# Decode attention with a parallel ReLU FFN: V on a second DMA queue, and weights instead of activations held stationary in the output products

## The chip, the cores and the metric

The kernel runs on one core of one Trainium2 chip. The metric is the device time of one execution in microseconds; the time before is the median of 3 runs. Lower is better.

## The reference

```python
x  = A_x                                   # (2, 1, 512) bf16
xn = layernorm(x)
q  = (xn @ wq).reshape(2, 1, 32, 128).transpose(0, 2, 1, 3)
s  = einsum("bhqd,bhkd->bhqk", q, k_cache) * 128 ** -0.5     # k_cache (2, 32, 8192, 128)
p  = softmax(s, axis=-1)
o  = einsum("bhqk,bhkd->bhqd", p, v_cache)
attn = o.transpose(0, 2, 1, 3).reshape(2, 1, 4096) @ wo      # wo (4096, 512)
ffn  = maximum(xn @ w1, 0) @ w2                              # w1 (512, 1792), w2 (1792, 512)
return x + attn + ffn                                        # (2, 1, 512) bf16
```

One token for each of 2 batch rows attends over 8192 cached keys in 32 heads. K and V are 128 MiB each, the weights 4 + 4 + 3.5 MiB. Everything is bf16.

## The kernel before, in words

The 64 (batch, head) combinations are taken in 32 pairs. One pair's K is one transfer of 4 MiB: 128 partitions, 64 for each head of the pair, each partition with 128 consecutive keys (32 KiB). V is laid out the same way. There are two buffers for K (`ks`) and two for V (`vs`); pair t uses buffer t % 2.

A step of PE (`step`, lines 337 to 361) does, for pair t: wait for K(t) (`dK`); 16 groups of 8 transposes of K tiles into PSUM (`tp`, L301); each group is copied to SBUF (`kT`, L416) by ACT (groups in `ON_ACT`) or DVE, and two groups later PE multiplies it with the pair's q (scores, L308, 64 moving columns). Then PE does the weighted sum with V of the pair before (`weighted`, L321), while DVE and ACT form the maximum and the exponentials of pair t. The first such sum, in pair 0, runs over a zero `prm`. ACT's part of a step (`pair`, lines 527 to 546) is: the kT copies, the maximum to SBUF (L533), two Exp activations with sums (L537), and, when PE has finished the weighted sum (`sW`), the copy of the result to `OTf` (L525). ACT runs its 32 pairs as a rolled loop of 16 rounds with two pairs each.

All large transfers are issued from SP's queue (lines 181 to 203), in this order: wq (L177, into `vs[1]`), w1, w2, K0, K1, V0; then, for t = 0 to 29: wait until PE has done the transposes of pair t, issue K(t+2); wait until PE has done the weighted sum of step t (`sW`), issue V(t+1). At last V31 in two halves (L196), wo in five pieces of 14, 7, 6, 3 and 2 blocks (L201, into the space of w1 and w2), and the store of the result (L166).

The prologue computes the layernorm, q (L247), FFN1 (L260, w1 stationary) and FFN2 (L278): there the ReLU result `hT` is stationary, 32 columns wide with the two batch rows 16 columns apart and zeros between, and w2 moves; the four 128-wide blocks of the output go to four column groups of the PE array, PSUM partitions 0, 32, 64, 96. Four more matmuls (L286) add x through `onex`, and the sum is kept in `ys` (128x128).

The tail, after step 31: row sums of the exponentials through `onesh` (L376), the weighted sum of V31 half by half (L321), division (L497, L501), transposes (L386), a selection product that puts o into the order of wo's rows (L391) and the copy to `OX` (L508), then wo (L405) in the same form as FFN2: `OX` stationary, 32 columns wide, wo moving, four column groups. DVE adds `ys` (L512), and SP stores 8 rows that lie 16 partitions apart.

Of the kernel before, what the change touches and what calls it, by code (L numbers as in the profile page):

```python
# [7 lines left out]
ALU = mybir.AluOpType  # L8
# [3 lines left out]
R = 2  # L12
# [7 lines left out]
def kernel(  # L20
# [13 lines left out]
    P = 128  # L34
    HP = P // 2
    bf16 = mybir.dt.bfloat16
    f32 = mybir.dt.float32

    Bsz, Sq, D = A_x.shape
# [3 lines left out]
    KT = D // P  # L43
# [3 lines left out]
    NP = N // 2  # L47
    WJ = H * Dh // P
# [8 lines left out]
    FJ = FT  # L57
    inv_sqrt = float(Dh) ** -0.5
    eps = 1e-5

    CT = P // KT
    CB = CT // Bsz
    assert KT * Bsz * CB == P
    ctx.enter_context(tc.tile_critical(no_gpsimd_drain=True))

    def sb(shape, dt, name):
        return ctx.enter_context(nc.sbuf_tensor(name, shape, dt))
# [14 lines left out]
    wo_sb = w_sb[:, 0:WJ * D].rearrange("p (j n) -> p j n", j=WJ)  # L82
    kT = [sb([P, EG, P], bf16, f"kT{i}") for i in range(4)]
    identb = sb([P, P], bf16, "identb")
    sel = sb([H, DQ, P], bf16, "sel")
    onesh = sb([P, 2, P], f32, "onesh")
    onesb = sb([1, P], bf16, "onesb")
# [19 lines left out]
    RD = sb([P, N], f32, "RD")  # L107
    OTn = sb([P, Bsz, H], bf16, "OTn")
    Ob = sb([H, Bsz, Dh], bf16, "Ob")
    OX = sb([P, WJ, CT], bf16, "OX")  # L110
    hT = sb([P, FJ, CT], bf16, "hT")
    ys = sb([P, P], f32, "ys")
    osb = sb([P, P], bf16, "osb")
    onex = sb([Bsz, CT], bf16, "onex")

    tp = [ps([P, EG, P], bf16, f"tp{i}") for i in range(4)]
    Sc = [ps([P, 512], f32, f"Sc{i}") for i in range(2)]
# [37 lines left out]
        "p (kt b) -> p kt b", b=Bsz  # L155
    )
    hp = ot[1][:, 0:FJ * Bsz].rearrange("p (j b) -> p j b", b=Bsz)
    y = Sc[1][:, 0:P]
    fin = ot[0][:, 0:P]

    def cols(ap, c):
        return ap[c * CT:(c + 1) * CT, :]


    def store(eng):
        eng.dma_start(  # L166
            out.rearrange("b s (c p) -> c (b s) p", p=P),
            osb[0:P - CB + 1:CB, :],
        ).then_inc(dO, 16)

    def load_k(t):
        nc.sync.dma_start(ks[t % R][:], K_all[t * P:(t + 1) * P, :]).then_inc(dK[t % R], 16)
# [1 line left out]
    def load_v(t):  # L174
        nc.sync.dma_start(vs[t % R][:], V_all[t * P:(t + 1) * P, :]).then_inc(dV[t % R], 16)
# [5 lines left out]
    @(lambda f: f(nc.sync))  # L181
    def _(sp):
        sp.dma_start(w1_sb, B_w1.rearrange("(p kt) f -> p kt f", kt=KT)).then_inc(dW1, 16)  # L183
        sp.dma_start(w2_sb, B_w2.rearrange("(p j) n -> p j n", j=FJ)).then_inc(dW2, 16)  # L184
        load_k(0)
        load_k(1)
        load_v(0)
        for t in range(NP - 2):
            sp.wait_ge(pT[NG - 1], t + 1)
            load_k(t + R)  # L190
            sp.wait_ge(sW, t + 1)
            load_v(t + 1)
        sp.wait_ge(sW, NP - 1)
        for i in range(2):
            sl = slice(i * SLOT // 2, (i + 1) * SLOT // 2)
            sp.dma_start(  # L196
                vs[(NP - 1) % R][:, sl], V_all[(NP - 1) * P:NP * P, sl]
            ).then_inc(dH[i], 16)
        for c in range(NC):
            sl = slice(cuts[c], cuts[c + 1])  # L200
            sp.dma_start(wo_sb[:, sl, :], wo_v[:, sl, :]).then_inc(dW[c], 16)  # L201
        sp.wait_ge(sE, 1)
        store(sp)


    @(lambda f: f(nc.gpsimd))
    def _(g):
        g.memset(identb[:], 0.0).then_inc(sG, 1)
        g.memset(sel[:], 0.0).then_inc(sG, 1)
        g.memset(onesh[:], 0.0).then_inc(sG, 1)  # L210
        g.wait_ge(sG, 1)
        g.affine_select(
            out=identb[:], in_=identb[:], compare_op=ALU.not_equal, fill=1.0,
            base=0, pattern=[[-1, P]], channel_multiplier=1,
        ).then_inc(sI, 1)
        g.wait_ge(sG, 2)
        g.affine_select(
            out=sel[:], in_=sel[:], compare_op=ALU.not_equal, fill=1.0,
            base=0, pattern=[[-1, DQ], [1, P]], channel_multiplier=-DQ,
        ).then_inc(sI, 1)  # L220
        g.wait_ge(sI, 2)
        g.memset(prm[0][:], 0.0).then_inc(sG, 1)
        g.wait_ge(sG, 4)
        for u in range(2):
            g.memset(onesh[u * HP:(u + 1) * HP, u, :], 1.0).then_inc(sI, 1)
            g.wait_ge(sI, 3 + u)
        g.memset(OX[:], 0.0).then_inc(sI, 1)
        g.wait_ge(sV, 100)
        for t in range(NP):
            if t >= R:  # L230
                g.wait_ge(sS, t - R + 1)
            g.tensor_copy(q2[t % R][:], qb[:, 2 * t:2 * t + 2]).then_inc(sQ1, 1)  # L232
        g.wait_ge(dO, 16).then_inc(sG, 1)
# [3 lines left out]
    def _(pe):  # L237
# [36 lines left out]
        pe.wait_ge(sF, 2)  # L274
        pe.wait_ge(dW2, 16)
        for j in range(FJ):
            for c in range(KT):
                pe.matmul(  # L278
                    cols(y, c),
                    lhsT=hT[:, j, :],  # L280
                    rhs=w2_sb[:, j, c * P:(c + 1) * P],
                    start=(j == 0),
                    stop=False,
                )
        for c in range(KT):
            i = pe.matmul(  # L286
                cols(y, c),
                lhsT=onex[:],
                rhs=xsb[:, c * P:(c + 1) * P],
                start=False,  # L290
                stop=True,
            )
        i.then_inc(sF, 1)

# [80 lines left out]
        for u in range(2):  # L375
            t = pe.matmul(dbp[:, :, u], lhsT=onesh[:, u, :], rhs=RS[:], start=True, stop=True)  # L376
        t.then_inc(sH, 1)
        for i in range(2):
            pe.wait_ge(dH[i], 16)
            for e in range(i * NG // 2, (i + 1) * NG // 2):  # L380
                weighted(1, e)
# [19 lines left out]
        for c in range(NC):  # L401
            pe.wait_ge(dW[c], 16)
            for j in range(cuts[c], cuts[c + 1]):
                for k in range(KT):
                    t = pe.matmul(  # L405
                        cols(fin, k),
                        lhsT=OX[:, j, :],
                        rhs=wo_sb[:, j, k * P:(k + 1) * P],
                        start=(j == 0),
                        stop=(j == WJ - 1),  # L410
                    )
        t.then_inc(sH, 1)

    def kcopy(eng, e):
        fn = eng.copy if e in ON_ACT else eng.tensor_copy
# [4 lines left out]
    def _(v):  # L420
        v.memset(eps_t[:], eps).then_inc(sV, 1)
        v.memset(onesb[:], 1.0)
        v.memset(xz[:], 0.0).then_inc(sZ, 1)
        v.memset(onex[:], 0.0)
        v.memset(hT[:], 0.0).then_inc(sZ, 1)
        v.memset(prm[R - 1][:], 0.0).then_inc(sP, 1)
        v.wait_ge(dX, 16)
        v.bn_stats(out=stats[:], in_=xsb[:]).then_inc(sV, 1)
# [12 lines left out]
            op1=ALU.mult,  # L441
        ).then_inc(sV, 1)
        v.wait_ge(sQ, 1)
        v.wait_ge(sI, 1)
        v.wait_ge(sZ, 1)
        v.tensor_copy(xz[:, :, Z:Z + Bsz], tpx).then_inc(sV, 1)
        v.wait_ge(sQ, 2)
# [1 line left out]
        v.tensor_scalar(  # L449
            out=qs[:], in0=qp, scalar1=inv_sqrt, scalar2=None, op0=ALU.mult  # L450
        ).then_inc(sV, 1)
        v.wait_ge(sZ, 2)
        v.tensor_copy(onex[:, 0:CT:CB], identb[0:Bsz, 0:Bsz])
        v.wait_ge(sF, 1)
        v.tensor_scalar(
            out=hT[:, :, 0:CT:CB], in0=hp, scalar1=0.0, scalar2=None, op0=ALU.max,
        ).then_inc(sF, 1)
        v.wait_ge(sQ, 3)

# [2 lines left out]
            tpq.rearrange("p l (g b) -> p l g b", b=Bsz),  # L462
        ).then_inc(sV, 93)
        v.wait_ge(sF, 3)
        v.tensor_copy(ys[:], y).then_inc(sF, 1)

        def pair(i, n):
            for e in range(NG):
# [18 lines left out]
        with v.Fori(0, NP // R):  # L487
# [16 lines left out]
        v.wait_ge(sH, 2)  # L504
        v.tensor_copy(Ob[:], tp[0][0:H, 0:Bsz, :]).then_inc(sV, 1)
        v.wait_ge(sH, 3)
        v.wait_ge(sI, 5)
        v.tensor_copy(  # L508
            OX[:, :, 0:CT:CB], Sc[1][:, 0:Bsz * WJ].rearrange("p (b j) -> p j b", b=Bsz)
        ).then_inc(sV, 1)  # L510
        v.wait_ge(sH, 4)
        v.tensor_tensor(out=osb[:], in0=fin, in1=ys[:], op=ALU.add).then_inc(sE, 1)  # L512


    @(lambda f: f(nc.scalar))
    def _(a):
        a.wait_ge(sV, 3)
        a.activation(
            out=rstd[:], in_=mv[:, 1:2], func=ACTF.Sqrt, bias=eps_t[:Bsz], scale=1.0
        ).then_inc(sA, 1)  # L520


        def out_copy(r, n, c):
            a.wait_ge(sW, n)
            a.copy(OTf[:, bass.ds(c, 2)], ot[r][:, 0:2]).then_inc(sO, 1)  # L525

        def pair(i, n, t):
            for e in range(NG):
                if e in ON_ACT:
                    a.wait_ge(pT[e], n)  # L530
                    kcopy(a, e)
            a.wait_ge(sB, n)
            a.copy(nm[i][:], bc_of(i)).then_inc(sN, 1)  # L533
            a.wait_ge(sN, n)
            for u in range(2):
                half = slice(u * HP, (u + 1) * HP)
                x = a.activation(  # L537
                    out=prm[i][half, :, u],
                    in_=S_of(i)[half, :, u],
                    func=ACTF.Exp,  # L540
                    bias=nm[i][half, u:u + 1],
                    scale=1.0,
                    accum_out=RS[half, bass.ds(t, 1)],
                )
            x.then_inc(sP, 1)
            out_copy(1 - i, n, t * 2)

        a.copy(nm[0][:, 0:1], eps_t[:]).then_inc(sO, 1)
        reg = nc.alloc_register(mybir.EngineType.Activation, "pairno_a")
        a.reg_mov(reg, 0)  # L550
        with a.Fori(0, NP // R) as tr:
            for r in range(R):
                a.reg_add(reg, reg, 1)
                pair(r, reg, tr * R + r)
# [1 line left out]
_INS = ['A_x', 'A_k_cache', 'A_v_cache', 'A_wq', 'A_wo', 'B_x', 'B_w1', 'B_w2']  # L556
_OUTS = [((2, 1, 512), 'bfloat16')]
# [25 lines left out]
```

## Time and profile before

| what | us |
|---|---|
| median of 3 runs (662.2 to 662.62) | 662.31 |
| the profiled execution's own time | 662.31 |
| its span in the profile | 660.24 |
| PE busy in the span | 557.1 |
| PE weight loads busy | 535.8 |
| DVE busy | 254.1 |
| ACT busy | 255.8 |
| mean granted TensorE clock | 0.935 |

An engine's busy time is the sum of its instructions' times in the span; PE and its weight loads overlap. The page cuts the span into 40 slices of 16.5 us and gives for each the busy share of the engines, of the 16 DMA engines, and the bytes moved. The timeline gives rows of "start us, duration us, engine, line, operation, out<-in, count", and in brackets how long the engine had been idle and what ended that. "SPq" and "ACTq" are DMA issues from the queue of that engine.

### The profile page before, as it was taken

Reading aid. Unit: us, or ns where it says so; the run is one execution under the profiler, and the core shown is the slowest. Engines: PE = TensorE matmul, PEld = TensorE weight load, DVE = VectorE, ACT = ScalarE, POOL = GpSimd, SP = SyncE. Lnnn points to the kernel's source line nnn. Section 1 sums busy time; section 2 is a strip of 40 time slices with the busy share of each in tenths; the row PEclk is TensorE's granted clock in tenths of the full one; section 3 lists DMA queues with packets and bytes.
Section 4 is the critical chain, followed back from the end, with each engine's and each line's share of the span. In section 5 each row is a group of like instructions: output and inputs, shape, how many; then the busy total and the mean of one; then the engine's idle time right before and its main releaser. Section 6 shows DMA issues by size and latency. Waiting matters only on the chain.

```text
span 660.2 us, 26934 instructions
## 1 busy us (share of the span) xinstructions
PE 557.1 (84%) x12774; PEld 535.8 (81%) x12774; DVE 254.1 (38%) x438; ACT 255.8 (39%) x403; POOL 9.5 (1%) x45
## 2 busy tenths in 40 slices
PE   1799899988789878879987978988878898887994
PEld 0498898978789878878987878888878898887993
DVE  1144354534344433334442433443434444343440
ACT  1034545433334434433353434435343443433430
POOL 2000000000000000000000000000000000000000
PEclk9789999989998988999897999988989998898996
DMA  8999999999999999999999999999999999999995
GB/s 362 435 439 424 430 433 431 437 427 433 429 433 435 429 435 425 433 439 429 435 425 433 437 429 437 425 433 435 431 437 425 433 435 431 433 427 435 431 424 242
DMA packets 10539, 280.67 MB, mean 425 GB/s; under 512 B 1182, under 2 KB 1184, under 8 KB 1696
## 3 DMA queue, kind: packets, MB, share of 16 engines
q1 hardware_dynamic: 10524, 280.50, 98.9%
q8 instruction: 9, 0.15, 0.1%
q14 instruction: 2, 0.02, 0.0%
q10 hardware_dynamic: 4, 0.00, 0.0%
HBM read 280.50 MB, written 0.00 MB: 425 GB/s over the span
## 4 chain that ended last, share of the span: by engine, by line
DMA 59%; PE 37%; ACT 2%; issue 1%; SPq 1%; ACTq 0%; DVE 0%
DMA ks<-in_A_k_cache_dram 54%; PE tp L301 21%; PE Sc L308 11%; PE ot L321 4%; DMA w_sb<-in_A_wo_dram 4%; ACT kT L416 2%; ACT L416 1%; SPq L201 0%; PE Sc L356 0%; SPq L196 0%; PE Sc L359 0%; PE ot L405 0%; SPq L184 0%; SPq L183 0%; SPq L177 0%
## 5 line engine op out<-in xcount | busy, mean ns | idle before, releaser
L301 PE MATMUL tp<-identb,ks 128*128 128x128 bf16 x4096 | 325.4, 229 | 71.7 <-DMA ks<-in_A_k_cache_dram 71.7
L416 DVE COPY kT<-tp 128x1024 bf16<-128x1024 bf16 x320 | 219.7, 691 | 328.4 <-PE tp L301 328.0
L301 PEld LDWEIGHTS tp<-identb,ks 128*128 128x128 bf16 x4096 | 256.7, 103 | 75.0 <-DMA ks<-in_A_k_cache_dram 75.0
L416 ACT COPY kT<-tp 128x1024 bf16<-128x1024 bf16 x192 | 194.3, 1012 | 235.3 <-PE tp L301 235.3
L308 PE MATMUL Sc<-q,kT 128*128 128x64 bf16 x4096 | 217.4, 196 | 6.6 <-ACT kT L416 5.6
L308 PEld LDWEIGHTS Sc<-q,kT 128*128 128x128 bf16 x4096 | 179.2, 100 | 10.1 <-ACT kT L416 8.8
L321 PE MATMUL ot<-prm,vs 128*128 128x64 bf16 x4224 | 156.3, 192 | 2.9 <-issue 2.3
L321 PEld LDWEIGHTS ot<-prm,vs 128*128 128x128 bf16 x4224 | 139.1, 97 | 5.8 <-issue 2.5
L533 ACT COPY nm<-Sc 128x2 f32<-128x2 f32 x32 | 5.1, 160 | 120.0 <-PE Sc L359 120.0
L537 ACT ACTIVATE prm<-Sc,nm 64x128 bf16<-64x128 f32 x64 | 25.8, 404 | 4.3
L475 DVE TENSOR_REDUCE mcol<-Sc 64x1 bf16<-64x128 f32 x64 | 18.6, 291 | 17.6 <-PE Sc L308 17.2
L416 ACT ACT_TABLE_LOAD x16 | 20.5, 1283 | 2.2
L247 PE MATMUL ot<-vs,xz 128*16 128x512 bf16 x32 | 9.3, 464 | 8.2 <-DMA vs<-in_A_wq_dram 8.2
L480 DVE TENSOR_REDUCE mx<-Sc 1x2 bf16<-1x128 bf16 x32 | 8.9, 279 | 16.9 <-PE Sc L356 16.9
L247 PEld LDWEIGHTS ot<-vs,xz 128*16 128x16 bf16 x32 | 3.3, 105 | 13.9 <-issue 11.5
L232 POOL COPY q<-qb 128x2 bf16<-128x2 bf16 x32 | 5.8, 184 | 588.6 <-PE Sc L308 566.1
L525 ACT COPY OTf<-ot 128x2 f32 x32 | 5.1, 160 | 22.4 <-PE ot L321 22.4
L537 ACT ACTIVATION_READ_ACCUMULATOR prm<-Sc,nm x64 | 11.8, 184 | 0.0
L405 PE MATMUL ot<-w_sb,OX 128*32 128x128 bf16 x128 | 4.3, 304 | 4.0 <-DMA w_sb<-in_A_wo_dram 3.9
L449 DVE TENSOR_SCALAR qs<-ot 16x512 bf16<-16x512 f32 x1 | 0.7, 678 | 17.4 <-PE ot L247 17.4
L405 PEld LDWEIGHTS ot<-w_sb,OX 128*32 128x32 bf16 x128 | 3.0, 133 | 5.2 <-DMA w_sb<-in_A_wo_dram 4.0
L356 PE MATMUL Sc<-identb,mcol 128*1 128x128 bf16 x32 | 7.0, 217 | 0.0
(55 smaller groups left out, 36.3 us busy)
## 6 DMA issues: line engine op xcount, KB each, us to landing
ks<-in_A_k_cache_dram SPq DMA_DIRECT2D x32, 4096.0 KB, 26.8
vs<-in_A_v_cache_dram SPq DMA_DIRECT2D x31, 4096.0 KB, 31.3
vs<-in_A_wq_dram SPq DMA_DIRECT2D x1, 4096.0 KB, 12.5
vs<-in_A_v_cache_dram SPq DMA_DIRECT2D x2, 2048.0 KB, 17.9
w_sb<-in_B_w_dram SPq DMA_DIRECT2D x2, 1792.0 KB, 18.2
w_sb<-in_A_wo_dram SPq DMA_DIRECT2D x1, 1792.0 KB, 23.9
w_sb<-in_A_wo_dram SPq DMA_DIRECT2D x1, 896.0 KB, 25.7
w_sb<-in_A_wo_dram SPq DMA_DIRECT2D x1, 768.0 KB, 27.1
```

What stands on the lines that cost most here:

```text
L232: g.tensor_copy(q2[t % R][:], qb[:, 2 * t:2 * t + 2]).then_inc(sQ1, 1)
L247: i = pe.matmul(qp, lhsT=xz[:, kt, Z - g * Bsz:Z - g * Bsz + QG * Bsz], rhs=vs[1][:, (kt * QG + g) * 512:(kt * QG + g + 1) * 512], start=( ...
L301: t = pe.transpose(tp[e % 4][:, i, :], ks[r][:, kk * Dh:(kk + 1) * Dh], identb[:])
L308: t = pe.matmul(Sc[r][:, 2 * kk:2 * kk + 2 * REP], lhsT=kT[e % 4][:, i, :], rhs=rep(q2[r][:]), start=True, stop=True,)
L321: t = pe.matmul(ot[r][:, 0:2 * REP], lhsT=vs[r][:, kk * Dh:(kk + 1) * Dh], rhs=rep(prm[r][:, kk, :]), start=(kk == 0), stop=(kk == KB - 1),)
L356: pe.transpose(tr_of(r), mcol[r][:], identb[:]).then_inc(sT, 1)
L405: t = pe.matmul(cols(fin, k), lhsT=OX[:, j, :], rhs=wo_sb[:, j, k * P:(k + 1) * P], start=(j == 0), stop=(j == WJ - 1),)
L416: fn(kT[e % 4][:], tp[e % 4][:]).then_inc(kR[e], 1)
L475: m = v.tensor_reduce(out=mcol[i][half, :], in_=S_of(i)[half, :, u], axis=AX.X, op=ALU.max)
L480: v.tensor_reduce(out=mx[i][:], in_=tr_of(i).rearrange("o (u m) -> o u m", u=2), axis=AX.X, op=ALU.max, negate=True,).then_inc(sX, 1)
L525: a.copy(OTf[:, bass.ds(c, 2)], ot[r][:, 0:2]).then_inc(sO, 1)
L537: x = a.activation(out=prm[i][half, :, u], in_=S_of(i)[half, :, u], func=ACTF.Exp, bias=nm[i][half, u:u + 1], scale=1.0, accum_out=RS[half ...
```

## The change

It has two parts. First, V1 to V30 are issued by ACT, at the end of each of its pairs, behind the copy to `OTf`; ACT's rolled loop has 15 rounds, and its last two pairs stand behind it without an issue. SP keeps K, V0, V31, the weights and the store. Second, the column groups go: FFN2 has the two columns of `hT` stationary and 512 columns of w2 moving, 14 matmuls, and DVE adds x when it copies the result to `ys` (2x512); wo has its own 128x128 blocks stationary and the two columns of `OX` moving, so the result lies transposed in PSUM (128 partitions, 4 blocks x 2 rows). `ys` is brought into the same PSUM sum by four f32 matmuls with a 2x2 identity (`ident2`), placed behind L376. Then DVE copies the sum to `yT`, PE transposes it to 8 rows, DVE copies these to `osb`, and SP stores 8 rows from 8 partitions. Zero fills of `OX`, `hT` and `onex` go.

```diff
@@ SP
         for t in range(NP - 2):
             sp.wait_ge(pT[NG - 1], t + 1)
             load_k(t + R)
-            sp.wait_ge(sW, t + 1)
-            load_v(t + 1)
...
         sp.wait_ge(sE, 1)
-        store(sp)
+        sp.dma_start(
+            out.rearrange("b s (c p) -> (b s c) p", p=P), osb[:]
+        ).then_inc(dO, 16)
@@ POOL
-        g.memset(OX[:], 0.0).then_inc(sI, 1)
+        g.memset(ident2[:], 0.0).then_inc(sG, 1)
+        g.wait_ge(sG, 5)
+        g.affine_select(
+            out=ident2[:], in_=ident2[:], compare_op=ALU.not_equal, fill=1.0,
+            base=0, pattern=[[-1, Bsz]], channel_multiplier=1,
+        ).then_inc(sI, 1)
@@ PE, FFN2
         for j in range(FJ):
-            for c in range(KT):
-                pe.matmul(
-                    cols(y, c),
-                    lhsT=hT[:, j, :],
-                    rhs=w2_sb[:, j, c * P:(c + 1) * P],
-                    start=(j == 0),
-                    stop=False,
-                )
-        for c in range(KT):
             i = pe.matmul(
-                cols(y, c),
-                lhsT=onex[:],
-                rhs=xsb[:, c * P:(c + 1) * P],
-                start=False,
-                stop=True,
+                y,
+                lhsT=hT[:, j, :],
+                rhs=w2_sb[:, j, :],
+                start=(j == 0),
+                stop=(j == FJ - 1),
             )
         i.then_inc(sF, 1)
@@ PE, tail
         t.then_inc(sH, 1)
+        for k in range(KT):
+            pe.matmul(
+                fin[:, k, :],
+                lhsT=ys[:, k * P:(k + 1) * P],
+                rhs=ident2[:],
+                start=(k == 0),
+                stop=False,
+            )
...
                 for k in range(KT):
                     t = pe.matmul(
-                        cols(fin, k),
-                        lhsT=OX[:, j, :],
-                        rhs=wo_sb[:, j, k * P:(k + 1) * P],
-                        start=(j == 0),
-                        stop=(j == WJ - 1),
+                        fin[:, k, :],
+                        lhsT=wo_sb[:, j, k * P:(k + 1) * P],
+                        rhs=OX[:, j, :],
+                        start=False,
+                        stop=(j == WJ - 1 and k == KT - 1),
                     )
         t.then_inc(sH, 1)
+        pe.wait_ge(sV, 106)
+        pe.transpose(
+            tp[1][0:Bsz * KT, 0, :], yT[:].rearrange("p b c -> p (b c)"), identb[:]
+        ).then_inc(sH, 1)
@@ DVE
         v.tensor_scalar(
-            out=hT[:, :, 0:CT:CB], in0=hp, scalar1=0.0, scalar2=None, op0=ALU.max,
+            out=hT[:], in0=hp, scalar1=0.0, scalar2=None, op0=ALU.max,
         ).then_inc(sF, 1)
...
         v.wait_ge(sF, 3)
-        v.tensor_copy(ys[:], y).then_inc(sF, 1)
+        v.tensor_tensor(out=ys[:], in0=y, in1=xsb[:], op=ALU.add).then_inc(sF, 1)
...
         v.wait_ge(sH, 4)
-        v.tensor_tensor(out=osb[:], in0=fin, in1=ys[:], op=ALU.add).then_inc(sE, 1)
+        v.tensor_copy(yT[:], ot[0][:, 0:KT * Bsz].rearrange("p (b c) -> p b c", c=KT)).then_inc(sV, 1)
+        v.wait_ge(sH, 5)
+        v.tensor_copy(osb[:], tp[1][0:Bsz * KT, 0, :]).then_inc(sE, 1)
@@ ACT
-        with a.Fori(0, NP // R) as tr:
+        with a.Fori(0, NP // R - 1) as tr:
             for r in range(R):
                 a.reg_add(reg, reg, 1)
                 pair(r, reg, tr * R + r)
+                a.dma_start(
+                    vs[1 - r][:], V_all[bass.ds((tr * R + r + 1) * P, P), :]
+                ).then_inc(dV[1 - r], 16)
+        for r in range(R):
+            a.reg_add(reg, reg, 1)
+            pair(r, reg, NP - R + r)
```

More of the change, by code (lines that the diff above doesn't have):

```diff
@@ L59 @@
     eps = 1e-5
-    CT = P // KT
-    CB = CT // Bsz
-    assert KT * Bsz * CB == P
     ctx.enter_context(tc.tile_critical(no_gpsimd_drain=True))
@@ L84 @@
     identb = sb([P, P], bf16, "identb")
+    ident2 = sb([Bsz, Bsz], f32, "ident2")
     sel = sb([H, DQ, P], bf16, "sel")
@@ L109 @@
     Ob = sb([H, Bsz, Dh], bf16, "Ob")
[L110 to L114, printed above, removed]
+    OX = sb([P, WJ, Bsz], bf16, "OX")
+    hT = sb([P, FJ, Bsz], bf16, "hT")
+    ys = sb([Bsz, D], f32, "ys")
+    yT = sb([P, Bsz, KT], bf16, "yT")
+    osb = sb([Bsz * KT, P], bf16, "osb")
     tp = [ps([P, EG, P], bf16, f"tp{i}") for i in range(4)]
@@ L157 @@
     hp = ot[1][:, 0:FJ * Bsz].rearrange("p (j b) -> p j b", b=Bsz)
[L158 to L169, printed above, removed]
+    y = Sc[1][0:Bsz, :]
+    fin = ot[0][:, 0:KT * Bsz].rearrange("p (b c) -> p c b", c=KT)
     def load_k(t):
@@ L423, in _ @@
         v.memset(xz[:], 0.0).then_inc(sZ, 1)
-        v.memset(onex[:], 0.0)
-        v.memset(hT[:], 0.0).then_inc(sZ, 1)
         v.memset(prm[R - 1][:], 0.0).then_inc(sP, 1)
@@ L443, in _ @@
         v.wait_ge(sQ, 1)
-        v.wait_ge(sI, 1)
         v.wait_ge(sZ, 1)
@@ L451, in _ @@
         ).then_inc(sV, 1)
-        v.wait_ge(sZ, 2)
-        v.tensor_copy(onex[:, 0:CT:CB], identb[0:Bsz, 0:Bsz])
         v.wait_ge(sF, 1)
         v.tensor_scalar(
-            out=hT[:, :, 0:CT:CB], in0=hp, scalar1=0.0, scalar2=None, op0=ALU.max,
+            out=hT[:], in0=hp, scalar1=0.0, scalar2=None, op0=ALU.max,
         ).then_inc(sF, 1)
@@ L506, in _ @@
         v.wait_ge(sH, 3)
-        v.wait_ge(sI, 5)
         v.tensor_copy(
-            OX[:, :, 0:CT:CB], Sc[1][:, 0:Bsz * WJ].rearrange("p (b j) -> p j b", b=Bsz)
+            OX[:], Sc[1][:, 0:Bsz * WJ].rearrange("p (b j) -> p j b", b=Bsz)
         ).then_inc(sV, 1)
         v.wait_ge(sH, 4)
-        v.tensor_tensor(out=osb[:], in0=fin, in1=ys[:], op=ALU.add).then_inc(sE, 1)
+        v.tensor_copy(yT[:], ot[0][:, 0:KT * Bsz].rearrange("p (b c) -> p b c", c=KT)).then_inc(sV, 1)
+        v.wait_ge(sH, 5)
+        v.tensor_copy(osb[:], tp[1][0:Bsz * KT, 0, :]).then_inc(sE, 1)
     @(lambda f: f(nc.scalar))
```

## The prediction

> **What bounds the kernel now.** I read the page from the top: the slices, the queues, the chain of waits.
>
> ```profile
> span 660.2 us, 26934 instructions
> ...
> DMA  8999999999999999999999999999999999999995
> GB/s 362 435 439 424 430 433 431 437 427 433 429 433 435 429 435 425 433 439 429 435 425 433 437 429 437 425 433 435 431 437 425 433 435 431 433 427 435 431 424 242
> ...
> q1 hardware_dynamic: 10524, 280.50, 98.9%
> ...
> DMA 59%; PE 37%; ACT 2%; issue 1%; SPq 1%; ACTq 0%; DVE 0%
> ```
>
> The sixteen DMA engines are busy from the first slice to the last; all the bytes come through one queue, SP's. The kernel is a stream of 280.5 MB, and the only time not paid by the stream is its head and what PE does after it. Two pairs follow each other at 19.43 us (K of the last two pairs starts PE at 606.18 and 625.62), so one 4 MB transfer takes 9.71. In the timeline the last rows of PE, DVE and the SP queue tell what stands behind the stream:
>
> ```profile
> 625.62 1.51 PE L301 MATMUL tp<-identb,ks 128*128 128x128 bf16 x24 [1.06 <-DMA ks<-in_A_k_cache_dram]
> ...
> 641.77 0.16 ACT L525 COPY OTf<-ot 128x2 f32 x1 [0.70 <-PE ot L321]
> ...
> 642.03 0.60 PE L376 MATMUL Sc<-RS,onesh 128*128 128x32 f32 x4 [0.38 <-issue]
> ...
> 645.14 2.13 PE L321 MATMUL ot<-prm,vs 128*128 128x64 bf16 x64 [0.55 <-DMA vs<-in_A_v_cache_dram]
> ...
> 648.50 0.42 DVE L508 CAST OX<-Sc 128x64 bf16<-128x64 f32 x1 [0.38 <-PE Sc L391]
> ...
> 649.52 1.60 PE L405 MATMUL ot<-w_sb,OX 128*32 128x128 bf16 x56 [1.05 <-DMA w_sb<-in_A_wo_dram]
> ...
> 655.74 1.04 PE L405 MATMUL ot<-w_sb,OX 128*32 128x128 bf16 x20 [1.41 <-DMA w_sb<-in_A_wo_dram]
> ...
> 656.84 0.29 DVE L512 TENSOR_TENSOR osb<-ot,ys 128x128 bf16<-128x128 f32 x1 [7.91 <-PE ot L405]
> 657.16 0.71 SPq L166 DMA_DIRECT2D out_dram<-osb  x1
> ```
>
> PE has OX at 648.92, before any of wo is in, and then waits for every piece of wo; after the last piece (656.4) some 0.4 us of matmuls, one DVE add and the store remain. K of pair 31, called K31 below, came at 625.6, with V30, V31 and wo still behind it in the same queue. PE's last step thus runs under 30 us of transfers. That cover is what the change touches.
>
> **The change, part by part.**
>
> *V on ACT's queue: the stream.* Bytes are the same and no slice has a hole to fill. As long as either queue has a transfer waiting, wo lands at 656.4 as now. The rate of two queues together is not shown by any row; the slices in mid-span lie between 424 and 439 GB/s around 432, and I bound the unknown by half a per cent either way, +-3 us, and take nothing: the single queue's 98.9% is the nearest row.
>
> *V on ACT's queue: the order.* This is the largest term. Now K and V land in the order in which PE uses them. With two queues K shares the engines with V, so K31 lands later and what lies behind it in the stream gets shorter. From both sides: if transfers were served in order of issue, K31 stays at 625.6; if all of V30 went first, K31 takes V30's place, 625.6 + 9.7 = 635.3. No row shows how two queues share; I take equal turns, packet by packet (the packet records show rows of 32 KB, 1.21 us each, eight per engine and transfer). The walk: K0 starts PE at 32.86, two transfers later, at 52.3, V0 is in.
>
> ```profile
> 46.10 0.33 SPq L172 DMA_DIRECT2D ks<-in_A_k_cache_dram  x1
> 52.50 0.33 SPq L175 DMA_DIRECT2D vs<-in_A_v_cache_dram  x1
> 64.46 0.33 SPq L172 DMA_DIRECT2D ks<-in_A_k_cache_dram  x1
> 70.93 0.33 SPq L175 DMA_DIRECT2D vs<-in_A_v_cache_dram  x1
> ```
>
> K2 (issued 46.10) starts at 52.3. V1 is issued behind ACT's OTf copy, 0.25 later than 52.50, and first bytes follow an issue by 1.0 to 1.3 us (wq 0.96 to 1.99, the store 657.16 to 658.5), so at about 54. K2 has two packets alone, six in turns: 52.3 + 2 x 1.21 + 12 x 1.21 = 69.3. V1 then has two left, done by 74.1; K3 (64.46) and V2 (70.93) are issued by then. From there neither queue runs empty, and each lands one transfer per 19.43: K31 at 69.3 + 29 x 19.43 = 632.8, V30 some 4.8 later. PE keeps up: K(t+2) is issued 11 to 13 us after K(t) lands, V(t+1) at most 18.4 + 1.5 after; V of the pair before is in 5 us after K and used 11 us after it.
>
> [...]
>
> *The issue on ACT.* 30 DMA issues of 0.33 (SP's rows) to 0.55 (ACT's own for xsb) stand behind the OTf copy and ahead of a table load (1.28, every second pair) and the first kT copy, for which PE's first scores wait. From pair 6 on PE waits 1.0 to 3.4 us for K at each step's start, and the table load at 603.20 ends 1.7 us before K lands: hidden, 0. Without that cover it would cost 30 x 0.4 = 12. In steps 2 to 4, where PE sets the pace, it moves them by up to 1.5 us; K4 lands at 108.1 by the walk, later than step 3 ends (103.9), so that is covered too. SP loses 30 issues and 30 waits; K's wait there is on PE (432.9 us in all), so nothing moves.
>
> *The prologue.* FFN2 becomes 14 matmuls of 512 columns, at L247's rate 0.21 (20 in 4.19) to 0.43 us: 3.0 to 6.0 in place of 1.7 + 0.3, from 26.73. PE has nothing to do until K0 at 32.86: hidden, 0; beyond the cover it would be 3 us. The memsets and the 2x512 add lie in the same gap.
>
> *The tail.* PE becomes its owner, so its terms add up from K31:
> 1. Step 31: 16.1 (625.6 to 641.7), 18.4 for the step before, 16.1 for the one before that; mean 16.9. 632.8 + 16.9 = 649.7.
> 2. To OX now: 641.7 to 648.92 is 7.2, less the 0.55 wait for V31's half, which has landed by then (645.1): 6.6. The four f32 matmuls of ys are new; L376's two are four rows in 0.60, so eight rows, 1.1. OX at 657.4, one us after wo is complete. V31's halves and all pieces of wo wait for PE, not the reverse.
> 3. wo: 128 matmuls, wo stationary (128x128), two columns moving. Rows with a full stationary tile: L321 64 in 2.12, 33 ns, contiguous; L260 56 in 3.52, 63 ns, two columns moving but the stationary read with a stride of 14. L278 (a 32-wide stationary) did 56 in 1.42, 25 ns. I take 33, since wo is contiguous as V is: 4.2, between 3.2 and 8.0. Ends 661.6.
> 4. New behind it: yT copy (0.16 as L501), transpose (0.25, two of them take 0.28 in L386), osb copy (0.2, under L505's 0.28) with three gaps of 0.05: 0.8. The old add (0.29 + 0.06) goes. PE's new wait for yT holds up nothing but this transpose. 662.4.
> 5. DVE's end to the end of the span: 657.13 to 660.24, 3.1. Eight rows of 256 bytes as before. 665.5.
>
> On term 3 the rows differ by their N and their stride at once. [...]
>
> **Sum.** The span goes from 660.24 to 665.5, +5.3. The profiled execution took 662.31 in all (2.07 outside the span), which is also the median of the three runs: 662.31 + 5.3 = **667.6**.
>
> **Rivals.**
> - *Order of issue, or K preferred* (the change then does not put V beside K in time): K31 at 625.6 or earlier, OX at 650, wo still binds at 656.4; the last eight matmuls are 0.3 and term 4 adds 0.5 net. 662.8. For it: K lands 27 us after its issue under a backlog, so order matters; against: two separate queues, nothing that shows a common order.
> - *Narrow matmuls are slow*: 63 ns a matmul as L260, 8.0 for term 3: 671.4. For it: L260 is the only row with two columns. Against: its stride.
> - *V first at every turn*: K31 at 635.3, 2.5 later: 670.1.
> - *Faster* (the other side): two queues move bytes at a higher rate in the bulk, because a packet of one starts under the end of the other's. Its place is the 600 us between K0 and the tail; 1% is worth 6.0, and 667.6 - 6.0 = 661.6 is still the same as before; it decides above 1.1% (6.6 us), since 661.0 is needed. At 1.5%: 658.6. Against: 98.9% busy, no slice above 439.
>
> **How the numbers follow.** 0.2% (1.3 us) is about what a measurement of this kernel can tell from no change. The forecast with its size errors (K31 +-2, step 31 16.1 or 18.4, rate +-3) has 0.60, and lies in 664 to 671; order of issue 0.13; narrow matmuls 0.13; V first 0.09; faster 0.05. Faster comes from the last, 0.05; same from the order of issue and a little of the forecast's low edge, 0.14; slower from the rest, 0.81. The range takes in the order of issue below and the narrow matmuls above, 662.7 to 672.0; outside are the faster case, and V first together with narrow matmuls.
>
> **What would show it.** Right: a second hardware queue with 30 x 4.19 = 126 MB; K31 starting PE near 633 with V30 landing some 5 us after it; the line of wo's matmuls with no idle time for DMA, in one block of about 4.2 us after OX near 657; GB/s slices unchanged up to 656. Wrong: K31 near 626 with wo's matmuls waiting for pieces (order of issue); a block of 8 us (narrow); slices above 437 all along (faster); or a PE idle time that ends on the kT copy from ACT at every step, which would mean that the issue on ACT is not covered.

## The result, and the profile after

The changed kernel takes **665.18 us** (median of 6 runs, 665.14 to 666.03) against 662.28 for the kernel before (6 runs); ratio 1.0046, 95% interval 1.0033 to 1.0059. It is 2.9 us slower. The forecast was slower by 5.3, 667.6. The profiled execution took 665.18, its span is 663.1.

The page of the changed kernel, the same parts as for before:

```profile
span 663.1 us, 26912 instructions
...
DMA  8999999999999999999999999999999999999994
GB/s 361 438 431 435 424 435 434 425 435 433 427 435 435 423 439 427 431 439 427 431 439 427 431 437 429 431 435 429 433 435 427 433 437 423 437 433 427 435 420 170
...
q1 hardware_dynamic: 6208, 154.67, 54.4%
q10 hardware_dynamic: 4324, 125.83, 44.1%
```

V is in the second queue, 126 MB, and the two together keep the engines as busy as one did (98.9% before, 98.5% now) at the same rate (432 and 431 GB/s in the two halves of 100 to 600 us; before 432 in both). In mid-span no stretch of the stream got better or worse; the last piece of wo landed at 655.12, where before it landed at 656.33. The difference in time is in the last 35 us. The timeline there (start us, duration, engine, line, operation, and in brackets the idle time before it and what ended it):

```profile
631.79 1.98 PE L286 MATMUL tp<-identb,ks 128*128 128x128 bf16 x24 [2.29 <-DMA ks<-in_A_k_cache_dram]
...
649.05 0.16 ACT L518 COPY OTf<-ot 128x2 f32<-128x2 f32 x1 [0.71 <-PE ot L306]
...
649.84 1.05 PE L364 MATMUL ot<-ident,ys 2*128 2x2 f32 x8
...
650.82 4.08 PE L306 MATMUL ot<-prm,vs 128*128 128x64 bf16 x128
...
656.14 0.23 DVE L499 CAST OX<-Sc 128x64 bf16<-128x64 f32 x1 [0.38 <-PE Sc L384]
...
656.42 3.36 PE L398 MATMUL ot<-OX,w_sb 128*128 128x2 bf16 x128 [0.32 <-DVE OX L499]
659.82 0.17 DVE L503 CAST yT<-ot 128x8 bf16<-128x8 f32 x1 [3.45 <-PE ot L398]
...
660.34 0.21 DVE L505 COPY osb<-tp 8x128 bf16<-8x128 bf16 x1 [0.36 <-PE tp L407]
660.58 0.37 SPq L190 DMA_DIRECT2D out_dram<-osb  x1
```

K31 starts PE at 631.79; before it was 625.62. PE then has no wait for DMA any more: V31's two halves are summed in one block of 128, wo's 128 matmuls run in one block. Before, the same two lines stood in pieces, with idle times between them that ended on a DMA. The end of the kernel has changed its owner, from the DMA engines to PE.

### The profile page after: what moved, and what is told of

It is laid out like the page before. It is cut to its first block, busy times and chain, and to the rows that moved or that the text cites. A ratio compares the mean times of both kernels' runs of the same rounds, so it can differ in the third digit from the quotient of the medians.

```text
span 663.1 us, 26912 instructions
## 1 busy us (share of the span) xinstructions
PE 562.3 (85%) x12737; PEld 538.2 (81%) x12737; DVE 253.3 (38%) x436; ACT 254.5 (38%) x402; POOL 8.9 (1%) x46
## 4 chain that ended last, share of the span: by engine, by line
DMA 61%; PE 35%; ACT 2%; issue 1%; ACTq 0%; SPq 0%; DVE 0%
DMA ks<-in_A_k_cache_dram 61%; PE tp L286 20%; PE Sc L293 10%; PE ot L306 3%; ACT kT L413 1%; PE ot L398 1%; ACT L413 0%; ACTq L548 0%; PE ot L364 0%; PE Sc L361 0%; PE Sc L341 0%; SPq L173 0%; PE Sc L344 0%; SPq L172 0%; SPq L166 0%
## 5 line engine op out<-in xcount | busy, mean ns | idle before, releaser
L518 ACT COPY OTf<-ot 128x2 f32 (+1 forms) x32 | 5.1, 160 | 27.8 <-PE ot L306 27.8
L472 DVE TENSOR_REDUCE mx<-Sc 1x2 bf16<-1x128 bf16 x32 | 8.9, 279 | 16.9 <-PE Sc L341 16.9
L530 ACT ACTIVATION_READ_ACCUMULATOR prm<-Sc,nm (+1 forms) x64 | 11.8, 185 | 0.0
L271 PE MATMUL Sc<-w_sb,hT 128*2 128x512 bf16 x14 | 5.8, 600 | 0.1
L344 PE MATMUL Sc<-mx,onesb 1*128 1x2 bf16 x32 | 5.5, 172 | 0.0
```

The lines of the kernel that those rows point to most:

```text
L271: i = pe.matmul(y, lhsT=hT[:, j, :], rhs=w2_sb[:, j, :], start=(j == 0), stop=(j == FJ - 1),)
L472: v.tensor_reduce(out=mx[i][:], in_=tr_of(i).rearrange("o (u m) -> o u m", u=2), axis=AX.X, op=ALU.max, negate=True,).then_inc(sX, 1)
L530: x = a.activation(out=prm[i][half, :, u], in_=S_of(i)[half, :, u], func=ACTF.Exp, bias=nm[i][half, u:u + 1], scale=1.0, accum_out=RS[half ...
```

## The experiments

Theory 1: two queues take turns on the DMA engines; K31 therefore comes 6 us later, PE owns the tail, and the new tail adds its length. Theory 2: the loss is the new form of the output products by itself. Theory 3: the DMA issues on ACT, or two queues as such, cost a little in every step. Each ratio is to executions of the kernel before that were timed beside the run; beside the first four runs their median was 662.2.

**V on ACT's queue alone.** The column groups stay.

```diff
-            sp.wait_ge(sW, t + 1)
-            load_v(t + 1)
...
+                a.dma_start(
+                    vs[1 - r][:], V_all[bass.ds((tr * R + r + 1) * P, P), :]
+                ).then_inc(dV[1 - r], 16)
```

> The kernel before with one part of the change alone: V1 to V30 from ACT's queue, output products in column groups as before. Theory 1 (two queues take turns, K31 comes 6 us late, PE owns the tail): K31 starts PE at 631.8 as in the changed kernel, step 31 ends at 649.0, OX 6.6 later without the f32 matmuls at 655.6, wo in one block of 128 x 28 ns = 3.6, add and store 3.5: span 662.7, +2.5 on before. Theory 2 (the loss is the new form of the output products): span 660.2 as before, within 0.5.

Measured: 662.68, ratio 1.0016 (1.0007 to 1.0025), span 660.6. Its timeline at the end:

```profile
631.44 2.00 PE L299 MATMUL tp<-identb,ks 128*128 128x128 bf16 x24 [2.29 <-DMA ks<-in_A_k_cache_dram]
...
654.70 0.42 DVE L506 CAST OX<-Sc 128x64 bf16<-128x64 f32 x1 [0.38 <-PE Sc L389]
...
655.18 1.97 PE L403 MATMUL ot<-w_sb,OX 128*32 128x128 bf16 x128 [0.52 <-DVE OX L506]
```

K31 is 6 us late here too, and OX comes at 655.1 as theory 1 says. But the whole of wo takes 1.97, not 3.6, so only 0.5 us is lost. I had taken 28 ns a matmul from before's wo line. The stretch tables (columns: stretch, its length, then PE, PEld, DVE, ACT and POOL busy, granted clock, DMA share, GB/s) show why that was no price: before first (the first 56 matmuls of wo, then the last 20), then this kernel.

```profile
649.50:651.10 1.60, 1.58 (x56) 1.35 (x56) 0.00 (x0) 0.00 (x0) 0.00 (x0) 0.55 1.01 415
...
655.00:657.00 2.00, 0.92 (x20) 0.38 (x20) 0.16 (x1) 0.00 (x0) 0.00 (x0) 0.50 0.02 8
```

```profile
655.10:657.20 2.10, 1.97 (x128) 1.80 (x128) 0.03 (x1) 0.00 (x0) 0.00 (x0) 1.00 0.03 8
```

The 28 ns were taken at a granted clock of 0.55; at 1.00 the same line does 15 ns a matmul. Most of this goes with the clock and not with the wait for a piece as such. The run with 32 more matmuls in the tail, further down, has the same line behind the same kind of wait at a granted clock of 1.00, 24 in 0.52 us or 22 ns a matmul; before, at 0.50, it was 24 in 0.83, 35 ns. Before first, then that run:

```profile
653.50 0.83 PE L405 MATMUL ot<-w_sb,OX 128*32 128x128 bf16 x24 [0.95 <-DMA w_sb<-in_A_wo_dram]
```

```profile
653.40 0.52 PE L407 MATMUL ot<-w_sb,OX 128*32 128x128 bf16 x24 [0.68 <-DMA w_sb<-in_A_wo_dram]
```

What decides which clock is granted is not shown.

**The form of the output products alone.** The changed kernel with V back on SP.

```diff
             load_k(t + R)
+            sp.wait_ge(sW, t + 1)
+            load_v(t + 1)
...
-                a.dma_start(
-                    vs[1 - r][:], V_all[bass.ds((tr * R + r + 1) * P, P), :]
-                ).then_inc(dV[1 - r], 16)
```

> The changed kernel with V1 to V30 back on SP's queue: the new form of the output products alone. Theory 1: K31 at 625.6, PE waits for the pieces of wo as before, the last 8 matmuls 0.3, yT, transpose and copy 0.8, store to end 2.6: 656.3 + 3.7 = 660.0, -0.2 on before (655.2 + 3.7 = 658.9 if wo lands as in the changed kernel). Theory 2: the loss stays, +2.9.

Measured: 660.87, ratio 0.9984 (0.9976 to 0.9993): faster than both kernels. In its timeline wo waits for its pieces again:

```profile
649.62 1.54 PE L400 MATMUL ot<-OX,w_sb 128*128 128x2 bf16 x56 [0.68 <-DMA w_sb<-in_A_wo_dram]
...
653.58 0.80 PE L400 MATMUL ot<-OX,w_sb 128*128 128x2 bf16 x24 [0.98 <-DMA w_sb<-in_A_wo_dram]
...
656.34 0.37 SPq L192 DMA_DIRECT2D out_dram<-osb  x1
```

The f32 matmuls and the slower wo are still there, under waits that end on DMA. Theory 2 falls: the same edits that cost 2.5 us on top of the first run (663.1 less 660.6) cost nothing here. The 2.5 consist of +0.35 because K31 came that much later than in the first run, +0.9 up to OX (the f32 matmuls, less a shorter copy), +1.4 for wo (3.36 for 1.97), +0.4 for what is new behind it and -0.5 from the store's issue to the end. The two parts do not add up: +0.5 and -1.3 alone, +2.9 together. (Some executions of before take about 660.9, as the last part of this section shows. Against those it is +1.8, 0 and +4.3, and they do not add up either.)

**The last two V back on SP.**

```diff
             load_k(t + R)
+            if t >= NP - 4:
+                sp.wait_ge(sW, t + 1)
+                load_v(t + 1)
...
-        with a.Fori(0, NP // R - 1) as tr:
+        with a.Fori(0, NP // R - 2) as tr:
```

> The changed kernel, but V29 and V30 are issued from SP's queue behind K30 and K31; V1 to V28 stay on ACT's queue. Theory 1 (only the order at the end of the stream costs): K31 is back at 624.5 to 626, span 659 to 660.5, 0 to -1 on before, though 28 of the 30 transfers still go by ACT. Theory 3 (two queues or the issue on ACT cost a little in every step): 28/30 of the loss stays, +2.7.

Measured: 660.92, ratio 0.9991 (0.9981 to 1.0001), span 658.8. K31 is back:

```profile
625.69 1.51 PE L289 MATMUL tp<-identb,ks 128*128 128x128 bf16 x24
```

With 28 of 30 transfers still on ACT's queue the whole loss is gone: the same form with no V on ACT's queue took 660.87. Theory 3 falls: neither the issue on ACT (0.34 us each) nor two queues cost anything that can be measured in the body. Only what is behind K31 in the stream counts.

**K and V both on ACT's queue.**

```diff
+            if more:
+                a.wait_ge(pT[NG - 1], n)
+                a.dma_start(
+                    ks[i][:], K_all[bass.ds((t + R) * P, P), :]
+                ).then_inc(dK[i], 16)
             a.wait_ge(sB, n)
```

> The changed kernel, but K2 to K31 also go by ACT's queue, issued by ACT behind its last kT copy of a step, so that K and V are in one queue in the order of use; SP keeps V31 and wo. Theory 1: K31 at 625.6 to 627 (V31 on SP's queue can share with its last microsecond), span 659 to 661. Theory 3 (the issue on ACT costs): 60 issues in place of 30, so the loss stays or doubles, +2.9 to +6.

Measured: 662.12, ratio 1.0009 (0.9998 to 1.002), no different from before, where the changed kernel took 665.18. K31 starts PE at 625.46. The loss neither stays nor doubles with sixty issues on ACT. It is still 1.25 more than the 660.87 of the same form with everything on SP's queue, and the profiled execution (661.06, span 658.9) is the fastest of its 12. One thing that I had only touched on may be the rest: V31 and wo, alone on SP's queue, now share with V30, and PE waits for V30 instead:

```profile
639.54 0.40 PE L303 MATMUL ot<-prm,vs 128*128 128x64 bf16 x8 [1.72 <-DMA vs<-in_A_v_cache_dram]
```

**How the queues share: rows of 16 KB.** Two runs, one with wq and V0 to V30 in two half-row transfers each, one with K so. The first is shown; K's is the same with `ks` and a second semaphore.

```diff
+                for h in range(2):
+                    sl = slice(h * HS, (h + 1) * HS)
                     a.dma_start(
-                    vs[1 - r][:], V_all[bass.ds((tr * R + r + 1) * P, P), :]
-                ).then_inc(dV[1 - r], 16)
+                        vs[1 - r][:, sl], V_all[bass.ds((tr * R + r + 1) * P, P), sl]
+                    ).then_inc(dVs[h][1 - r], 16)
```

> The changed kernel, with wq and V0 to V30 as two transfers of half a row (16 KB) each in place of one of 32 KB; K keeps rows of 32 KB. If the queues take turns packet by packet, K moves two bytes for each of V while both wait; K is ahead and V lands last: PE waits for V at the weighted sums, step 31 ends near 646.5 in place of 649.0, OX near 654, wo's block of 3.4 ends near 657.4: span 660.7, -2.4 on the changed kernel's 663.1. If the queues share by bytes or serve in order of issue, nothing moves: 663.1.

> The changed kernel, with K as two transfers of half a row (16 KB); V keeps 32 KB. Turns by packet: V moves two bytes for each of K, V30 is in before K31, and K31 lands at 635.5, just ahead of V31 and wo: +3.7 on the changed kernel, span 666.8. Shares by bytes: 663.1.

Measured: V in halves 665.16, ratio 1.0044 (1.0029 to 1.006), span 663.7; K in halves 671.36, ratio 1.0138 (1.0122 to 1.0153), span 669.3. First V in halves, then K in halves:

```profile
628.54 0.41 PE L316 MATMUL ot<-prm,vs 128*128 128x64 bf16 x8 [2.62 <-DMA vs<-in_A_v_cache_dram]
...
633.40 1.50 PE L296 MATMUL tp<-identb,ks 128*128 128x128 bf16 x24
```

```profile
637.95 1.93 PE L291 MATMUL tp<-identb,ks 128*128 128x128 bf16 x24 [2.32 <-issue]
```

In the last line PE waits for the second half of K31, which landed at 637.86, though the row says "issue". The order moved the way that turns by packet give, and shares by bytes do not: with small V packets PE no longer waits for K but for V (K31 landed at 626, 7 us before PE came to it); with small K packets V30 landed 3.8 us ahead of K31, and K31 came 6 us later than in the changed kernel. The sizes were off: the first did not gain the 2.4 us, and the second lost 6.2 where 3.7 was expected. By the landing records the last piece of wo came 2.7 and 3.9 us later than in the changed kernel, so the stream itself is slower with half rows (430 to 431 GB/s in mid-span for 431 to 432). That is of the size of both misses (step 31 ended at 649.4, 646.5 expected; 2.5 in the second run), but that it is their cause is not shown separately.

The packet records of the changed kernel show the turns themselves. They do not name the DMA engine, but where exactly one packet starts as another ends, the two can be taken to be on one engine. From 100 to 600 us 1088 such pairs are found; in 944 the second packet is of the other queue. In these records a packet of 32 KB takes 1.22 us, and one of 16 KB in the two runs above 0.61: a queue with half rows moves half as much in its turn.

**The stride of w1.** `(j f)` for `(f j)` in FFN1's stationary tiles, w2's rows to match.

```diff
-        w1_v = w1_sb[:].rearrange("p kt (f j) -> p kt j f", j=FJ)
+        w1_v = w1_sb[:].rearrange("p kt (j f) -> p kt j f", j=FJ)
```

> The changed kernel with FFN1's stationary tiles contiguous in SBUF (w1's columns taken block by block, w2's rows loaded to match, in runs of 1 KB). 56 matmuls of two columns: 3.5 us as now if two moving columns make them slow, 1.5 (26 ns each, the rate of wo's line in the changed kernel) if the stride of the stationary read does. The span does not depend on it: 663.1, a few tenths more if w2's short runs slow the stream.

Measured: 667.18 in one run, span 665.1. The changed kernel's FFN1, then this one's:

```profile
22.82 3.52 PE L254 MATMUL ot<-xz,w_sb 128*128 128x2 bf16 x56
```

```profile
22.31 1.55 PE L254 MATMUL ot<-xz,w_sb 128*128 128x2 bf16 x56
```

It was the stride: 63 ns with columns 28 bytes apart, 28 ns with columns side by side. The granted clock differed too, 0.82 over the first block and 1.00 over the second, but it is not the reason: within the first block it fell from 1.00 to 0.50, and the matmuls started every 60 ns throughout (every 25 in the second). Why the stride costs time is not shown. The 2 us of span are more than the few tenths expected; w2 in runs of 1 KB is slower to load (it landed 1 us later, and K0 starts PE at 33.90, also 1 us later, with PE idle for 6.58 before it). K31 landed 1.9 us later, the last of wo 0.95, and I did not follow the rest.

**Why the form alone was faster.** In before's profile the fourth piece of wo came 2.2 us after the third, here 1.0; the packet records show a 16 KB packet of the instruction queue just then (653.48 to 654.59). Eight of the last piece's 128 packets, a sixteenth, as one of the 16 DMA engines would have, ended one after the other between 655.35 and 655.91, all others by 654.57. The packets of the instruction queue keep step with PE: in before seven of them ended between 29.51 and 73.25, and PE started 1600 matmuls and weight loads between the first and the last, 267 to a packet; the next packet comes behind the loop, at 647.03. That makes some 61 bytes each, so 32 matmuls with their weight loads would be near 4 KB of PE's program and 64 near 8, an estimate. Theory 4: this load of PE's program holds back the last pieces. The next run lengthens the program ahead of the loop, the two after it lengthen it behind the loop.

```diff
-        for kt in range(KT):
-            i = pe.transpose(tpx[:, kt, :], xn[:, kt, :], identb[0:Bsz, 0:Bsz])
+        for _ in range(17):
+            for kt in range(KT):
+                i = pe.transpose(tpx[:, kt, :], xn[:, kt, :], identb[0:Bsz, 0:Bsz])
```

> The kernel before, with the four transposes of xn done 17 times, 64 more matmuls in PE's idle time before wq lands; nothing else. In the profile of before the fourth piece of wo lands 2.2 us after the third where 1.0 is its share, and a packet of 16 KB of PE's program runs on one DMA engine just then (1.1 us). Theory 4 (this program load delays the last pieces; where it falls depends on the program's length): total 661.0 in place of 662.2, with the pieces 1.0 apart. If the delay belongs to the column form itself: 662.2 as before.

Measured: **715.73**, ratio 1.0815 (1.0788 to 1.0841). From the page of this kernel, its queues and its costliest group:

```profile
q8 instruction: 72, 1.18, 0.7%
...
L302 PE MATMUL tp<-identb,ks 128*128 128x128 bf16 x4096 | 325.0, 229 | 101.8 <-issue 95.6
```

Every kernel above has 9 such packets; this one has 72, again and again through the loop, and PE stands still on "issue" for up to 13.8 us at a time. 64 matmuls in idle time, ahead of the loop, made the loop load its program anew. It is not the length of the program alone: with 64 more behind the loop, two runs on, there are 9 again. Whether it is the number of instructions ahead of the loop or the place at which the loop then begins is not shown. The run answers nothing about the last pieces of wo.

```diff
         t.then_inc(sH, 1)
+        for _ in range(32):
+            pe.matmul(Sc[1][:, 0:2], lhsT=identb[:], rhs=identb[:, 0:2], start=True, stop=True)
         for i in range(2):
             pe.wait_ge(dH[i], 16)
```

> The kernel before with 32 idle matmuls of two columns behind L376, outside the loop: 0.9 us on PE, covered by its waits for V31's half (0.55) and for the pieces of wo (3.9), so nothing by themselves. They move wo's matmuls 4 KB on in PE's program, so that the load of the next 16 KB of program falls some 1 to 2 us elsewhere against the last pieces of wo. Theory 4 (in the kernel before that load holds one DMA engine back for 1.1 us while the last two pieces come in): 661.0 if it leaves them, with the last pieces 1.0 and 0.6 apart; 662.2 if the load has nothing to do with it.

> The same with 64 idle matmuls (1.8 us of PE, still under the 4.4 us of waits): 8 KB on in the program. Theory 4: the load falls at another point of the tail again, 661.0 where it is clear of the last pieces; 662.2 otherwise.

Measured: 32 more, 662.2, ratio 0.9997 (0.9988 to 1.0006); 64 more, 662.94, ratio 1.0015 (1.0006 to 1.0024). In the profile with 64 more the pieces are in (the last landed at 654.98), and PE itself stands in the middle of wo, as it did for 1.65 in the sum of V31; each time a 16 KB packet of the instruction queue had ended 1.4 us before PE went on. From the one stop to the other PE ran 128 matmuls (13, 2, 4 and 109) with their weight loads, 256 instructions to a packet of 16 KB:

```profile
656.77 0.46 PE L407 MATMUL ot<-w_sb,OX 128*32 128x128 bf16 x19 [2.03 <-issue]
```

The profiled execution with 32 more had its last pieces 0.9 and 0.7 us apart and took 660.73; most of its other executions took 662.0 to 662.5. Before does the same: of the 35 executions timed beside the first four runs six took 660.7 to 661.3, the rest 661.6 to 662.8. The form alone stayed within 660.65 and 661.01 in all 11. So one program can end either way, about 1.3 us apart. That the program load decides it is what before's packet records suggest. But a load does not always hold a piece back: in the first run one ran from 652.64 to 653.71, while wo was still coming in, and no packet of the last piece ended after 654.37. The two runs do not show it, and it stays open. The gain of the form alone over before is of just this size.

## Why the prediction was right, point by point

- *The stream.* The forecast took the rate of the single queue: right, 431 to 432 GB/s in mid-span, and no time gained. wo was in at 655.12 where 656.4 was forecast, because the late last piece of before did not recur; PE came after it all the same.
- *The order.* K31 at 632.8 was forecast, 631.79 measured. The walk put K2, K3 and K4 at 69.3, 88.7 and 108.1; they landed at 69.58, 87.78 and 107.20, so the 1.0 was gained there, and from then on K came every 19.43 as forecast. V30 landed 4.9 us after K31 (4.8 forecast), but this agreement is luck: up to the pair before, V came 7.3 us after K, not 4.8. Behind K31 come the halves of V31, whose rows are 16 KB. By the packet times V30's last three packets then need 3 x 1.21 + 2 x 0.61 = 4.85, an estimate. The turns by packet, taken without a row to show them, are borne out by the half-row runs and the packet records; and with the last two V back on SP K31 is back at 625.7 and the loss gone. This was the step that carried the forecast.
- *The issue on ACT.* 0.34 us each, hidden; no loss with 28 issues on ACT (660.92, and 660.87 for the same form with none).
- *The prologue.* FFN2 took 5.78 us, near the upper end of 3.0 to 6.0, and ended half a microsecond before K0. Hidden, barely. The two ends of the range are two clocks: here the granted clock was 0.55 from 26.4 to 32.5, and in the run with w1's stride changed, at 1.00, the same 14 matmuls took 3.18. First the changed kernel, then that run:

```profile
26.62 5.78 PE L271 MATMUL Sc<-w_sb,hT 128*2 128x512 bf16 x14
...
32.93 1.51 PE L286 MATMUL tp<-identb,ks 128*128 128x128 bf16 x24 [0.53 <-DMA ks<-in_A_k_cache_dram]
```

```profile
24.14 3.18 PE L271 MATMUL Sc<-w_sb,hT 128*2 128x512 bf16 x14
```

- *The tail.* PE owned it. Step 31: 16.9 forecast, 17.3 measured (631.79 to 649.05 with the copy's wait). To OX: 7.7 forecast, 7.3 measured, the eight f32 rows at 1.05 for 1.1. wo: 4.2 forecast, 3.36 measured, 26 ns a matmul; this is the largest of the terms that were too long. The forecast took L321's 33 ns because both are contiguous, but L321 moves 64 columns and wo two. Its 25 ns for L278 (56 in 1.42) is the row of the weight loads; the matmuls took 1.69, 30 ns. The sum does not use it. Behind it 0.8 and 0.77. To the end of the span 3.1 forecast, 2.5 measured: the store's issue takes 0.37 with rows on adjacent partitions, 0.71 with rows 16 partitions apart, a gain that I had put at nothing.
- *The sum.* K31 -1.0, step 31 +0.4, to OX -0.4, wo -0.8, the end -0.6: 665.5 becomes 663.1 within rounding. All of the miss is size; the path was the one forecast.
- *The rivals.* Order of issue, V first and faster are out by K31's place and the rate; narrow matmuls by 26 ns, with the stride as the reason for L260's 63.

What the prediction did not say outright is that the two parts meet: the form costs 2.5 us only where the order has made PE the last, and nothing where wo is still waited for.

## What to carry to other kernels

In a kernel bound by one stream of transfers, count what stands behind the last load that a long step needs. Here the second queue did not change the rate (431 to 432 GB/s in mid-span either way), but it took turns with the first by packet (944 of 1088 pairs), and so K31 came 6.2 us later and the cover was gone from everything after it. It was enough to keep the last two V in one queue with K (660.92 against 665.18). Price an edit under the owner that the stage will have after the change, and look up the granted clock of every row from which a matmul rate is taken: the column groups did 28 ns at 0.55 and 15 at 1.00.

## What the runs showed that I had not expected

- 64 small matmuls more ahead of a rolled loop cost 53 us: 72 loads of 16 KB of program in place of 9, and PE idle for up to 13.8 us at a time. A few instructions more in front of a large loop can have a price of their own.
- Stationary tiles read with a stride of 28 bytes took 63 ns a matmul, contiguous ones 28 ns.
- The column groups did wo in 1.97 us at the full granted clock, 15 ns a matmul; before, at a granted clock of 0.50 to 0.55, the same line needed 28 ns and more.
- With half rows of 16 KB for V or for K the last piece of wo landed 2.7 or 3.9 us later.
